# The end of a windowed-attention and MLP kernel: the guard's sum, the last tile's cut and ScalarE's branch

## The chip, the cores and the metric

The kernel runs on one core of a Trainium2 chip. The core has TensorE (matrix multiplication, with its weight loads listed apart), VectorE, ScalarE, GpSimd and SyncE; each has its own queue of instructions and they meet through semaphores. DMAs are issued from the queues of SyncE, ScalarE and GpSimd and run on 16 DMA engines. The metric is device time in microseconds (us), lower is better. Times of single steps come from one profiled execution, in us from the start of its span.

## The reference

Four batches of 768 rows, 8 heads of 64 columns, attention over a window of 128 keys and 4 sink keys, then a layer norm, two matrices with a ReLU between them, and the sum with the attention's output:

```python
keep = is_sink | in_window              # n_sink = 4, window = 128
scores = np.where(keep, scores, -1e9)   # scores = q k^T / 8
a = np.exp(scores - max);  a = a / (sum(a) + 1e-9)
x = (a @ v)                             # heads side by side: [4, 768, 512]
xn = (x - mu) / np.sqrt(var + 1e-6) * g_ln
out = x + np.maximum(xn @ w_ch1, 0) @ w_ch2     # 512 -> 2048 -> 512
```

## The kernel before

The 3072 rows are 24 tiles of 128 rows, handled as 12 chunks of 256. A chunk passes through loads, transposes, scores, exponentials, the product with v, the norm, and the two layers of `mlp(c)`. No maximum is subtracted before the exponential. The kernel instead keeps the reciprocals of all row sums in `rec` (128 x 24 x 8) and at the end counts those outside 1e-9 to 1e9. If the count is zero, the result stands; otherwise the slow routine `general` computes everything again. That count is the **guard**.

The order of the instructions is not written out by hand. Each step is given to a planner as `P.op(name, engines with estimated times, priority, code, reads, writes)`. The planner simulates the engines, gives each step the moment at which its inputs, its engine and its buffers are free, and the steps are then emitted in order of planned start. Each engine works through its own steps in that order. Buffers come from rings; the ring `one` has four PSUM banks, and a step that writes to a new buffer of it must wait until the last user of a bank is done with it.

The end of the program is what the change touches:

- The second layer of a tile is 16 matmuls that add up in one bank, in four steps `pc{t}{f}_{s}` of four (line 1074). VectorE then writes `ot`, the sum with the attention's output (step `o{t}{f}`, line 1083), and a store goes out (line 1087). For the last tile, number 23, the 512 columns are divided by `LAST_CUTS` into two halves with matmuls, sum and store of their own; the first half's store is issued by ScalarE, the second's by SyncE.
- `guard` (lines 1114 to 1116, VectorE) leaves one count for each partition in `n_bad`. `gsum` (line 1119) adds them over the partitions by a matmul with a column of ones into a bank of the ring `one`. `gflag` (line 1121, VectorE) copies the sum as an integer to `flag`.
- `hold` (line 1125) is a matmul that reads the last column of the last output tile. It keeps TensorE from going on before that tile is summed.
- `nc.values_load(flag)` (line 1159) loads the flag into a register of every engine, and `tc.If` (line 1161) has each engine compare and branch over `general`. The last store of SyncE, `order_last`, is emitted behind that load. Hints at the program's start mark the branch as likely taken for TensorE, ScalarE and GpSimd.
- Behind the branch come the waits and barriers that end the program (line 1196 in the trace). SyncE waits there for one semaphore after the other, those of the stores among them.

Of the kernel before, what the change touches and what calls it, by code (L numbers as in the profile page):

```python
# [7 lines left out]
FP32 = mybir.dt.float32  # L8
BF16 = mybir.dt.bfloat16
AF = mybir.ActivationFunctionType  # L10
ALU = mybir.AluOpType
# [185 lines left out]
def pe(us):  # L197
    return {"PE": (us, us + Plan.PE_DRAIN)}


def act(n):
    t = 0.065 + 0.000833 * n
    return (t, t + 0.105)


def dve(n, per=1.04):
    t = 0.067 + 0.001 * per * n
    return (t, t + 0.09)


def fix(occ, extra=0.09):
    return (occ, occ + extra)
# [12 lines left out]
SW_Q = (0.25, 0.7, 0.9)  # L225

LOW, HIGH = 1e-9, 1e9
LAST_CUTS, LAST_ACT = (0, 256, 512), (3,)
NEG = -1e30
NEVER = -1e9  # L230
BIG = 3.3e38
# [138 lines left out]
def kernel(  # L370
# [12 lines left out]
    nc = tc.nc  # L383
# [6 lines left out]
    DM = moe_w_ch1.shape[0]  # L390
# [3 lines left out]
    NT = B * RB  # L394
    NC = B * RC
# [7 lines left out]
    P = Plan()  # L403
# [26 lines left out]
    def const(name, shape, dtype):  # L430
        return consts.tile(shape, dtype, name=name)
# [14 lines left out]
    w2 = [const(f"w2_{c}", [128, 4, DM], BF16) for c in range(4)]  # L446
    junk = nc.const_aps.tensor(1.0, [128, 512], BF16)
    rec, low = const("rec", [128, NT, H], FP32), const("low", [128, NT, H], FP32)
    n_bad, flag = const("n_bad", [128, 1], FP32), const("flag", [1, 1], mybir.dt.int32)
    g_s, g_r = const("g_s", [128, H, NS], FP32), const("g_r", [128, 3, H], FP32)  # L450
    ones_f = const("ones_f", [128, 1], FP32)
# [3 lines left out]
    Bc = {n: Buf(n) for n in names}  # L455
# [4 lines left out]
    def constant(name, eng, us, prio, emit, reads=(), **kw):  # L460
        return P.op(name, {eng: fix(us)}, prio, emit, reads=[Bc[r] for r in reads], **kw)

    V, G = nc.vector, nc.gpsimd
# [4 lines left out]
        out=ident_f, in_=ident_f, compare_op=ALU.not_equal, fill=1.0, base=0,  # L468
        pattern=[[-1, 128]], channel_multiplier=1), rw=[Bc["ident_f"]])
    constant("up1", "POOL", 0.3, -98, lambda e: G.affine_select(  # L470
        out=upper, in_=upper, compare_op=ALU.is_ge, fill=0.0, base=0,
# [36 lines left out]
    def negs(e):  # L508
# [7 lines left out]
        out=sel.rearrange("p (a b h) -> p a b h", a=2, b=2),  # L516
        in_=ident.rearrange("p (a b t h s) -> p t a b h s", a=2, b=2, h=2, s=NS)[:, 0],
        op=ALU.add, axis=mybir.AxisListType.X), ["ident"], writes=[Bc["sel"]])
# [8 lines left out]
         writes=[gr_b], dma=HW_T)  # L527
    P.op("gtt", pe(0.1), PAR["gtt"], lambda e: nc.tensor.transpose(gt_p.t[:, 0:NDM], g_rows, ident_f[0:NDM, 0:NDM]),
         reads=[gr_b, Bc["ident_f"]], writes=[gt_p])
    P.op("gtc", {"DVE": fix(0.07)}, PAR["gtt"] + 0.1, lambda e: V.tensor_copy(gt, gt_p.t[:, 0:NDM]), reads=[gt_p], writes=[Bc["gt"]])  # L530
    for h in range(H):
# [3 lines left out]
            reads=[Bc["vc"]], writes=[Bc["vcd"]], nb=3.5 + 0.55 * h)  # L535
    for b in range(B):
# [4 lines left out]
            reads=[Bc["vcd"], Bc["vc"], Bc["sel4" if b else "sel"]], writes=[Bvs[b]], nb=PAR["vs0"][1] if b == 0 else 40.0 * b)  # L541
# [7 lines left out]
    for c in range(4):  # L549
        sl = slice(512 * c, 512 * (c + 1))  # L550
        P.op(f"w1ld{c}", {"POOL": (0.75, 0.8)}, w1prio[c], lambda e, c=c, sl=sl: G.dma_start(
            w1[c], moe_w_ch1[:, sl].rearrange("(j p) n -> p j n", p=128)), writes=[Bw1[c]], dma=SW_W)
    for c in range(4):
        P.op(f"w2ld{c}", {"POOL": (0.75, 0.8)}, PAR["w2p"][c], lambda e, c=c: G.dma_start(
            w2[c], moe_w_ch2[512 * c:512 * (c + 1), :].rearrange("(t p) n -> p t n", p=128)),
            writes=[Bw2[c]], dma=SW_W)
# [471 lines left out]
    def mlp(c):  # L1028
        T = 16.0 * c + 8.0
# [3 lines left out]
        for u in range(NH1 // 2):  # L1033
# [8 lines left out]
            def mm(e, u=u, ph=ph):  # L1042
                for s in range(2):
                    ht = 2 * u + s
                    for j in range(NDM):
# [4 lines left out]
            o = P.op(f"ph{c}_{u}", pe(0.944 if by_tile else 0.872), pr, mm_t if by_tile else mm, reads=[xnt_t[2 * c + u % 2] if by_tile else xnt, (Bw1 if c < PAR["x_by_dma"] else Bw1g)[u // 2]],  # L1050
                     writes=[ph], hold=[hb, xnt])
# [10 lines left out]
        for i in range(2):  # L1062
            t = 2 * c + i
            b, r = t // RB, t % RB
            ot, st, rs, x = Buf(f"ot{t}", "ot"), xst_b[t], xst_b[t, "rs"], x_b[t]
            cuts = LAST_CUTS if t == NT - 1 else (0, DM)
            for f in range(len(cuts) - 1):
                pc, wd = Buf(f"pc{t}{f}", "one"), cuts[f + 1] - cuts[f]
                sl = slice(cuts[f], cuts[f + 1])
                for s in range(4):  # L1070
                    def mm(e, s=s, i=i, pc=pc, sl=sl, wd=wd):
                        for ii in range(4):
                            ht = 4 * s + ii
                            nc.tensor.matmul(pc.t[:, 0:wd],  # L1074
                                             lhsT=(h1[2 * s + i].t[:, 128 * ii:128 * ii + 128] if by_tile else
                                                   h1[ht // 2].t[:, 256 * (ht % 2) + 128 * i:256 * (ht % 2) + 128 * i + 128]),
                                             rhs=w2[s][:, ii, sl], start=ht == 0, stop=ht == NH1 - 1)
                    P.op(f"pc{t}{f}_{s}", pe(0.865 * wd / DM), T + 4 * i + s + 4 * f + 0.5, mm,
                         reads=[*([h1[2 * s + i]] if by_tile else h1[2 * s:2 * s + 2]), Bw2[s]], **({"writes": [pc]} if s == 0 else {"rw": [pc]}))
                oo = Buf(f"oo{t}{f}")  # L1080
                tail["ot"], tail["oo"] = ot, oo
                P.op(f"o{t}{f}", {"DVE": dve(wd, 1.14)}, T + 4 * i + 3.5, lambda e, sl=sl, pc=pc, wd=wd, ot=ot, st=st, x=x:
                     V.scalar_tensor_tensor(ot.t[:, sl], in0=pc.t[:, 0:wd], scalar=st.t[:, 16:17],  # L1083
                                            in1=x.t[:, sl], op0=ALU.mult, op1=ALU.add),
                     reads=[pc, st, rs, x], writes=[ot, oo])
                P.op(f"st{t}{f}", {"ACT" if len(cuts) - f in LAST_ACT else "SP": (0.54, 0.59)}, T + 4 * i + 3.6,
                     lambda e, sl=sl, ot=ot, b=b, r=r: (nc.sync if e == "SP" else nc.scalar).dma_start(
                         out[b, 128 * r:128 * (r + 1), sl], ot.t[:, sl]),
                     reads=[ot, oo], dma=HW_S)

    last_use, tail = {}, {}
# [11 lines left out]
    for c in range(NC):  # L1103
        mlp(c)
        if c == PAR["x_by_dma"] - 1:
            for s in range(4):
                for j in range(NDM):
# [3 lines left out]
                         reads=[Bw1[s], Bc["gt"]], writes=[Bw1g[s]], after=last_use[s])  # L1111

    def guard(e):
        V.tensor_scalar(low, rec, LOW, HIGH, op0=ALU.max, op1=ALU.min)
        V.tensor_tensor(low, low, rec, op=ALU.not_equal)
        V.tensor_reduce(out=n_bad, in_=low, op=ALU.add, axis=mybir.AxisListType.XY)
    nb_b, pt_f, fl_b = Buf("n_bad"), Buf("ptf", "one"), Buf("flag")
    P.op("guard", {"DVE": fix(0.9)}, 1000.0, guard, reads=recs, writes=[nb_b])
    P.op("gsum", pe(0.06), 16.0 * NC + 0.7, lambda e: nc.tensor.matmul(
        pt_f.t[0:1, 0:1], lhsT=n_bad, rhs=ones_f, start=True, stop=True), reads=[nb_b, Bc["ones_f"]], writes=[pt_f])  # L1120
    P.op("gflag", {"DVE": fix(0.1)}, 1000.0, lambda e: V.tensor_copy(flag, pt_f.t[0:1, 0:1]),
         reads=[pt_f], writes=[fl_b])

    hl = Buf("hold", "one")
    P.op("hold", pe(0.06), 1000.0, lambda e: nc.tensor.matmul(
        hl.t[0:1, 0:1], lhsT=tail["ot"].t[:, DM - 1:DM], rhs=ones_f, start=True, stop=True),
        reads=[tail["ot"], tail["oo"], Bc["ones_f"]], writes=[hl])

    order = P.run()

# [2 lines left out]
    t = PAR["t0"]  # L1133
    for o in order:
# [6 lines left out]
        if n > 0:  # L1141
            free = [(max([e_ for b_, e_ in banks[i].lives if b_ < t], default=0.0), i) for i in range(8)
                    if all(e_ < t or b_ > o.start + 0.3 for b_, e_ in banks[i].lives)]
            if free:
                i = min(free)[1]
                sizes = [512] * (n // 2) + [256] * (n % 2) if cold else [256] * n
                items.append((t + 0.001, -1, (sizes, pairs[i // 2][:, i % 2, :] if i < 4 else ones[i - 4])))
        t = o.start + occ * (2 if cold and not o.name.startswith("pm") else 1)
# [52 lines left out]
```

## Time and profile before

| | |
|---|---|
| time, median of 3 runs | 216.89 us (216.62 to 217.34) |
| the profiled execution: time | 217.02 us |
| the profiled execution: span, first to last instruction | 215.5 us |
| granted TensorE clock | 1.00 throughout |
| TensorE busy | 205.9 us, 96% of the span |
| VectorE, ScalarE, GpSimd busy | 53%, 51%, 52% |

In the rows below PE is TensorE's matmuls, PEld its weight loads, DVE VectorE, ACT ScalarE, POOL GpSimd and SP SyncE. A q behind the name (ACTq) marks an instruction of the engine's sequencer: a wait, a branch, a load of a register, the issue of a DMA. A row of the timeline has start, length, engine, line, operation, output<-inputs, shape and count; in brackets stands the idle time before it and what ended it. A row of a source line has the least, median and greatest length in ns and the first and last start. A matmul's listed length includes its way through the array, so matmuls overlap and their pace is read from their starts.

### The profile page before, as it was taken

The numbers are of one execution on the slowest core, as the hardware profiler recorded it, in microseconds if no ns is written. First come the engines' busy times: TensorE is split into PE (matmuls) and PEld (weight loads), VectorE is DVE, ScalarE is ACT, GpSimd is POOL, SyncE is SP. The second block draws the span as 40 slices with busy tenths as digits, with TensorE's granted clock in tenths as the row PEclk, the third lists the DMA queues.
The fourth block names the chain that finished last, engine by engine and source line by source line (L and its number), as shares of the span: only waits on it lengthen the run. The fifth ranks groups of instructions, "written<-read, shape, count | busy, mean of one in ns | idle before, by whom it ended". The sixth has DMA issues, their size and how long they took to land.

```text
span 215.5 us, 6660 instructions
## 1 busy us (share of the span) xinstructions
PE 205.9 (96%) x2743; PEld 144.1 (67%) x2765; DVE 115.3 (53%) x315; ACT 110.0 (51%) x178; POOL 111.8 (52%) x166
## 2 busy tenths in 40 slices
PE   7798899999999999999999999999999999999994
PEld 2467875765865875864865865864865865865853
DVE  5589875698445446446345446446355345444011
ACT  3796387496562562562562562562562562530610
POOL 7978632499972881871971981871971211201000
PEclk9999999999999999999999999999999999999999
DMA  5999999999999999799799899899799302202103
GB/s 156 187 190 205 193 206 192 167 180 132 154 187 169 123 125 145 87 175 151 123 115 170 112 147 145 111 122 168 111 141 149 80 3 76 73 0 76 49 2 105
DMA packets 104554, 28.04 MB, mean 130 GB/s; under 512 B 94788, under 2 KB 101576, under 8 KB 104520
## 3 DMA queue, kind: packets, MB, share of 16 engines
q0 software_dynamic: 69872, 13.18, 90.2%
q1 hardware_dynamic: 33448, 13.74, 35.7%
q10 hardware_dynamic: 1200, 0.66, 1.1%
q8 instruction: 22, 0.36, 0.7%
q14 instruction: 12, 0.10, 0.2%
HBM read 27.43 MB, written 6.29 MB: 156 GB/s over the span
## 4 chain that ended last, share of the span: by engine, by line
PE 88%; DVE 5%; DMA 3%; issue 2%; ACT 1%; ACTq 0%; DVEq 0%
PE one L1074 39%; PE one L1046 36%; PE pair L980 3%; DMA natf<-in_q_dram 3%; PE one L953 2%; PE one L960 2%; PE one L969 1%; DVE st L881 1%; DVE xnt L909 1%; PE one L988 1%; PE one L1039 1%; DVE x L873 1%; DVE xc L885 1%; PE pair L605 1%; PE pair L730 1%
## 5 line engine op out<-in xcount | busy, mean ns | idle before, releaser
L1074 PE MATMUL one<-w,h 128*128 128x512 bf16 (+1 forms) x378 | 84.5, 371 | 2.2 <-issue 1.6
L1056 ACT ACTIVATE h<-one 128x512 bf16<-128x512 f32 x93 | 55.6, 598 | 47.3 <-PE one L1046 42.6
L1046 PE MATMUL one<-xnt,w 128*128 128x256 bf16 x704 | 79.3, 273 | 0.0
L1046 PEld LDWEIGHTS <-w 128*128 128x128 bf16 x704 | 68.6, 98 | 10.4
L1074 PEld LDWEIGHTS <-h 128*128 128x128 bf16 x400 | 37.3, 98 | 39.6
L998 ACT ACTIVATE pe<-pair 128x768 bf16<-128x768 f32 x36 | 27.2, 809 | 41.0 <-PE pair L980 41.0
L645 POOL DMA_DIRECT2D vn<-in_v_dram x59 | 38.7, 695 | 10.9 <-DMA w<-in_moe_w_ch_dram 6.8
L890 POOL TENSOR_SCALAR st<-st 128x1 f32<-128x1 f32 x24 | 8.9, 369 | 62.4 <-DVE st L883 61.9
L1021 DVE RECIPROCAL rec<-one 128x4 f32<-128x4 f32 x36 | 6.4, 178 | 62.5 <-PE one L969 51.1
L1083 DVE SCALAR_TENSOR_TENSOR ot<-one,st,x 128x512 f32<-128x512 f32 (+1 forms) x25 | 18.2, 727 | 13.9 <-PE one L1074 9.0
L891 POOL TENSOR_TENSOR st<-st,mhalf 128x1 f32<-128x1 f32 x24 | 17.0, 707 | 2.0
L881 DVE BATCH_NORM_STATS2 st<-x 128x6 f32<-128x512 bf16 x24 | 16.7, 695 | 0.8
L1023 DVE TENSOR_TENSOR x<-one,rec 128x256 bf16<-128x256 f32 x36 | 15.3, 425 | 1.2
L703 POOL DMA_DIRECT2D nat<-in_k_dram x16 | 14.9, 932 | 1.9 <-DMA natp<-in_q_dram 1.6
L703 POOL DMA_DIRECT2D nat<-in_q_dram x16 | 14.3, 905 | 0.0
L1003 DVE TENSOR_TENSOR pe<-pe,band 128x768 bf16<-128x768 bf16 x24 | 12.2, 552 | 0.0
L885 DVE TENSOR_SCALAR xc<-x,st 128x512 bf16<-128x512 bf16 x24 | 9.3, 387 | 0.9
L980 PE MATMUL pair<-qT,kT 64*64 64x128 bf16 (+1 forms) x528 | 9.2, 204 | 0.0
L953 PEld LDWEIGHTS <-pe 128*128 128x128 bf16 (+1 forms) x144 | 6.2, 97 | 2.9 <-issue 0.8
L778 ACT ACTIVATE pe<-pair 128x1024 bf16<-128x1024 f32 (+1 forms) x8 | 7.1, 916 | 1.8 <-PE pair L730 1.4
L1039 PE MATMUL one<-xnt,w 128*128 128x128 bf16 x128 | 8.0, 220 | 0.0
L980 PEld LDWEIGHTS <-kT 64*64 64x64 bf16 x528 | 7.2, 108 | 0.4 <-ACT w L1110 0.4
(112 smaller groups left out, 165.7 us busy)
## 6 DMA issues: line engine op xcount, KB each, us to landing
out_dram<-ot SPq DMA_DIRECT2D x23, 256.0 KB
w<-in_moe_w_ch_dram POOLq DMA_DIRECT2D x8, 512.0 KB, 14.5
nat<-in_k_dram POOLq DMA_DIRECT2D x16, 128.0 KB, 5.1
nat<-in_q_dram POOLq DMA_DIRECT2D x16, 128.0 KB, 5.6
vn<-in_v_dram POOLq DMA_DIRECT2D x44, 32.0 KB, 6.0
vn<-in_v_dram POOLq DMA_DIRECT2D x15, 64.0 KB, 6.3
natp<-in_k_dram POOLq DMA_DIRECT2D x3, 256.0 KB, 14.3
vn<-in_v_dram POOLq DMA_DIRECT2D x6, 128.0 KB, 9.2
```

What stands on the lines that cost most here:

```text
L645: P.op(f"vld{t}_{i}", {"POOL": (0.8, 0.85)}, prio + 0.001 * i, lambda e, p0=p0, n=n, hs=hs, src=src: G.dma_start(m.t[p0:p0 + n, hs, 0:64], ...
L703: lambda e, nat=nat, ap=ap: G.dma_start(nat.t, ap), writes=[nat], dma=SW, after=gate(c))
L881: P.op(f"bn{t}", {"DVE": fix(0.60)}, d + 0.12, lambda e: V.bn_stats(st.t[:, 8:14], x.t), reads=[x], writes=[st, mv])
L891: G.tensor_tensor(st.t[:, 16:17], st.t[:, 17:18], mhalf, op=ALU.pow)),
L980: nc.tensor.matmul(pps[u].t[64 * g:64 * g + 64, h2, col + c0:col + c0 + n], lhsT=kt.t[rs, hp, k0:k0 + 64], rhs=qT.t[rs, hp, q0:q0 + n], st ...
L998: nc.scalar.activation(pes[j].t.rearrange("p a b -> p (a b)")[:, 0:768].rearrange("p (a b) -> p a b", a=2), pps[j].t[:, :, 0:384], AF.Exp, ...
L1003: V.tensor_mul(at_s, at_s, band[j] if r > 1 else edge[r][j].unsqueeze(1).to_broadcast([128, 4, 192]))
L1023: P.op(f"x{t - 1}{u}", {"DVE": dve(256)}, d + 0.051 + 0.002 * u, lambda e, u=u, rc=rc, pv=pv: V.tensor_tensor(x.t[:, 256 * u:256 * u + 256 ...
L1046: nc.tensor.matmul(ph.t[:, 256 * s:256 * s + 256], lhsT=w1[ht // 4][:, j, 128 * (ht % 4):128 * (ht % 4 + 1)], rhs=xnt.t[:, j, :], start=j ...
L1056: nc.scalar.activation(hb.t, ph.t, AF.Relu)
L1074: nc.tensor.matmul(pc.t[:, 0:wd], lhsT=(h1[2 * s + i].t[:, 128 * ii:128 * ii + 128] if by_tile else h1[ht // 2].t[:, 256 * (ht % 2) + 128 ...
L1083: V.scalar_tensor_tensor(ot.t[:, sl], in0=pc.t[:, 0:wd], scalar=st.t[:, 16:17], in1=x.t[:, sl], op0=ALU.mult, op1=ALU.add),
```

## The change

Three things are changed, all at the end of the program.

1. The guard's counts are no longer added by TensorE. A DMA issued by GpSimd (`gmove`) moves the 128 counts from 128 partitions into one row of one partition, and VectorE reduces that row and copies it to `flag` (`gflag`). This step is placed behind the sum of tile 22 (`after=[tail["sum", NT - 2]]`).
2. The last tile's second layer is divided at column 320 instead of 256: the first part has 320 columns, the second 192.
3. ScalarE gets a copy of one element of the last output tile (`hold_act`), behind which its load of the flag and its branch stand.

```diff
-LAST_CUTS, LAST_ACT = (0, 256, 512), (3,)
+LAST_CUTS, LAST_ACT = (0, 320, 512), (3,)
...
+    n_bad_t, n_sum, act_end = const("n_bad_t", [1, 128], FP32), const("n_sum", [1, 1], FP32), const("act_end", [1, 1], FP32)
...
-                P.op(f"o{t}{f}", {"DVE": dve(wd, 1.14)}, T + 4 * i + 3.5, lambda e, sl=sl, pc=pc, wd=wd, ot=ot, st=st, x=x:
+                tail["sum", t] = P.op(f"o{t}{f}", {"DVE": dve(wd, 1.14)}, T + 4 * i + 3.5, lambda e, sl=sl, pc=pc, wd=wd, ot=ot, st=st, x=x:
...
-    nb_b, pt_f, fl_b = Buf("n_bad"), Buf("ptf", "one"), Buf("flag")
+    nb_b, fl_b = Buf("n_bad"), Buf("flag")
     P.op("guard", {"DVE": fix(0.9)}, 1000.0, guard, reads=recs, writes=[nb_b])
-    P.op("gsum", pe(0.06), 16.0 * NC + 0.7, lambda e: nc.tensor.matmul(
-        pt_f.t[0:1, 0:1], lhsT=n_bad, rhs=ones_f, start=True, stop=True), reads=[nb_b, Bc["ones_f"]], writes=[pt_f])
-    P.op("gflag", {"DVE": fix(0.1)}, 1000.0, lambda e: V.tensor_copy(flag, pt_f.t[0:1, 0:1]),
-         reads=[pt_f], writes=[fl_b])
+    nt_b = Buf("n_bad_t")
+    P.op("gmove", {"POOL": (0.8, 0.85)}, 1000.0, lambda e: G.dma_start(n_bad_t[0:1, :], n_bad[:, 0:1]),
+         reads=[nb_b], writes=[nt_b], dma=SW_Q)
+    def total(e):
+        V.tensor_reduce(out=n_sum, in_=n_bad_t, op=ALU.add, axis=mybir.AxisListType.X)
+        V.tensor_copy(flag, n_sum)
+    P.op("gflag", {"DVE": fix(0.2)}, 1000.0, total, reads=[nt_b], writes=[fl_b], after=[tail["sum", NT - 2]])
...
+    P.op("hold_act", {"ACT": act(1)}, 1001.0, lambda e: nc.scalar.copy(act_end, tail["ot"].t[0:1, DM - 1:DM]),
+         reads=[tail["ot"], tail["oo"]], writes=[Buf("hold_act")])
```

## The prediction

> **What bounds the kernel now.** I read the page first (engines, chain), then the chain of waits and the timeline of the last 11 us, then the rows of the exit (flag loads, branches, end waits), then the DMA shares of that stretch.
>
> ```profile
> span 215.5 us, 6660 instructions
> PE 205.9 (96%) x2743; PEld 144.1 (67%) x2765; DVE 115.3 (53%) x315; ACT 110.0 (51%) x178; POOL 111.8 (52%) x166
> PE 88%; DVE 5%; DMA 3%; issue 2%; ACT 1%; ACTq 0%; DVEq 0%
> ```
>
> TensorE is busy 96% of the span and carries 88% of the chain. The diff touches nothing ahead of the guard's counting (L1116 at 194.3 us), so every term lies in the end. The timeline there, in order (start, length, engine, line):
>
> ```profile
> 194.01 0.69 POOL L891 TENSOR_TENSOR st<-st,mhalf 128x1 f32<-128x1 f32 x1
> 194.32 0.35 DVE L1116 TENSOR_REDUCE n_bad<-low 128x1 f32<-128x192 f32 x1
> 195.78 2.32 PE L1074 MATMUL one<-w,h 128*128 128x512 bf16 x10
> 197.94 7.15 PE L1046 MATMUL one<-xnt,w 128*128 128x256 bf16 x64
> 205.19 0.60 ACT L1056 ACTIVATE h<-one 128x512 bf16<-128x512 f32 x1 [0.28 <-PE one L1046]
> 205.36 0.60 PE L1074 MATMUL one<-w,h 128*128 128x512 bf16 x2
> 205.88 0.09 PEld L1119 LDWEIGHTS one<-ones_f,n_bad 128*1 128x1 f32 x2 [0.42 <-ACT h L1056]
> 206.01 6.26 PE L1074 MATMUL one<-w,h 128*128 128x512 bf16 x44
> 206.11 0.15 DVE L1121 CAST flag<-one 1x1 int32<-1x1 f32 x1 [7.16 <-PE one L1119]
> 208.86 0.75 DVE L1083 SCALAR_TENSOR_TENSOR ot<-one,st,x 128x512 f32<-128x512 f32 x1 [2.61 <-PE one L1074]
> 210.72 0.48 DVE L1083 SCALAR_TENSOR_TENSOR ot<-one,st,x 128x256 f32<-128x256 f32 x1 [1.11 <-PE one L1074]
> 211.24 0.38 ACTq L1087 DMA_DIRECT2D out_dram<-ot  x1
> 212.37 0.48 DVE L1083 SCALAR_TENSOR_TENSOR ot<-one,st,x 128x256 f32<-128x256 f32 x1 [1.16 <-PE one L1074]
> 212.88 0.34 SPq L1087 DMA_DIRECT2D out_dram<-ot  x1
> ```
>
> TensorE runs without a gap to 212.27 except around the guard's matmul (L1119); the last sum, `o231`, follows, and SyncE issues the last store at 212.88. What comes behind it is in the rows of the exit: flag loads (L1159), branches (L1161), end waits (L1196; its SyncE row asked for in two stretches).
>
> ```profile
> L1159 POOLq TENSOR_LOAD <-flag x1: 498/498/498, 206.3 to 206.3; - x1
> L1159 SPq TENSOR_LOAD <-flag x1: 516/516/516, 210.0 to 210.0; - x1
> L1159 SPq SEQ_ASSERT  x1: 37/37/37, 210.8 to 210.8; - x1
> L1159 ACTq TENSOR_LOAD <-flag x1: 473/473/473, 211.7 to 211.7; - x1
> L1161 ACTq COMPARE_BRANCH  x1: 68/68/68, 212.2 to 212.2; - x1
> L1161 ACTq EVENT_SEMAPHORE  x1: 17/17/17, 212.7 to 212.7; - x1
> L1196 ACTq DRAIN  x1: 8/8/8, 212.8 to 212.8; - x1
> L1196 POOLq DRAIN  x1: 1380/1380/1380, 208.3 to 208.3; - x1
> L1196 SPq EVENT_SEMAPHORE  x11: 28/28/28, 213.8 to 214.4; - x11
> L1196 SPq EVENT_SEMAPHORE  x1: 28/28/28, 214.6 to 214.6; - x1
> L1196 SPq DRAIN  x1: 13/13/13, 214.7 to 214.7; - x1
> L1196 POOLq EVENT_SEMAPHORE  x4: 17/17/17, 214.8 to 215.4; - x4
> ```
>
> SyncE makes twelve end waits. Eleven run from 213.8 to 214.4, 0.06 us apart; the twelfth, for the last store, is at 214.6 and not 214.5. SyncE drains at 214.7, GpSimd's barrier follows at 214.8, the span ends at 215.5. ScalarE was there at 212.8, GpSimd at 208.3 + 1.4 = 209.7. So the end is set by last sum, last store and SyncE's waits, and those two have slack.
>
> **The change, part by part.**
>
> *The guard's matmul goes.* The two matmuls ahead of it end at 205.96. One of 512 columns lasts 0.38 (row below), so the second began at 205.58. They start 0.216 apart ((2.32 - 0.38)/9 in the row of 195.78), so the next would begin at 205.80; it began at 206.01. Saved: 0.21. The guard's weight load waited for ScalarE's 205.19 + 0.60 = 205.79, which frees the PSUM bank it wrote to. The matmul behind it accumulates in a bank already held, on hidden blocks written long ago. If it had to wait for that same release, it would start at 205.88, where the guard's load did: 0.13 saved. Bounds 0.13 to 0.22; a loss is excluded, since TensorE gets no instruction in place of these. I take 0.21, because that wait belongs to the bank.
>
> *Cut at 320.* TensorE's time for the last tile must not grow: 16 matmuls of 320 and 16 of 192 for 32 of 256.
>
> ```profile
> L1074 PE MATMUL one<-w,h x378: 272/379/391, 30.9 to 212.0; 128*128 128x512 bf16 x173, 128*128 128x256 bf16 x16
> 22.77 1.95 PE L1039 MATMUL one<-xnt,w 128*128 128x128 bf16 x32
> ```
>
> The row of L1074 holds the lengths: 272 ns is the 256-column one, 379 the 512. Starts are 0.109 apart at 256 columns ((7.15 - 0.27)/63), 0.216 at 512: 0.42 ns a column. At 128 they are at most 0.061 apart (1.95/32), so the weight loads, one a matmul, allow at least that and 192 columns take 0.082 by the line, 0.085 at most (midway between 0.061 and 0.109). Old and new are both 3.49 us; at worst 16 x 0.003 = 0.05 is lost. I take 0, since the line holds to within 0.008 at 128. The last sum shrinks: 0.75 at 512 and 0.48 at 256 columns is 1.04 ns a column, so 64 fewer save 0.07 (bounds 0.05 to 0.08 by the rounding of the rows). The first sum moves 16 x 64 x 0.42 ns = 0.43 later and is 0.07 longer: from 210.72 - 0.21 + 0.43 = 210.94 to 211.49. ScalarE's store issue, 0.38, then ends at 211.9; nothing waits for it before the end. `o231` starts at 212.16 and ends at 212.58, the store is issued at 212.61 instead of 212.88.
>
> *A smaller last store*, 96 for 128 KB. The DMA shares by stretch (the last two numbers are the share and GB/s):
>
> ```profile
> 213.25:213.65 0.40, 0.00 (x0) 0.00 (x0) 0.00 (x0) 0.00 (x0) 0.00 (x0) 1.00 0.05 20
> 213.65:214.25 0.60, 0.00 (x0) 0.00 (x0) 0.00 (x0) 0.00 (x0) 0.00 (x0) 1.00 0.71 232
> 214.70:215.50 0.80, 0.00 (x0) 0.00 (x0) 0.00 (x0) 0.00 (x0) 0.00 (x0) 1.00 0.11 20
> ```
>
> The store's packets fill 213.65 to 214.25; a quarter less is at most 0.15. SyncE can use only the 0.1 by which its twelfth wait is late; after that its own row of waits is next. Bounds 0 to 0.1. I take 0.08, near the upper end, as the byte share exceeds it.
>
> *GpSimd's DMA, and VectorE's sum and copy.* `n_bad` is ready at 194.67, GpSimd free at 194.70. Its other small DMAs:
>
> ```profile
> L645 POOL DMA_DIRECT2D vn<-in_v_dram x59: 610/677/829, 29.9 to 159.1; - x59
> DMA to landing us min/median/max: 4.0/6.1/13.3
> ```
>
> So GpSimd spends 0.6 to 0.9 and the row lands between 198.7 and 208.0. Nothing stands behind it on GpSimd but the flag load. VectorE takes it up behind the sum of tile 22, which now ends at 209.61 - 0.21 = 209.40. The reduction of 128 elements lies between the cast (0.15) and the reduction of 192 (0.35), the copy is 0.15: flag at 209.7 to 209.9. VectorE is idle there for 1.11, now 1.54. SyncE loads the flag at about 209.9 as before and is through in 0.85; its store comes at 212.6. GpSimd's exit lasts 206.3 to 209.7, 3.4, so it ends at 213.3; the barrier wants it at 214.3. Cost 0, hidden by 0.9 us of slack. Without that cover each microsecond by which the flag is late costs one.
>
> *ScalarE behind a copy.* A copy of one element: 0.2 (row below), no second table load in the run, though casts, Exp and Relu all ran.
>
> ```profile
> L474 ACT ACT_TABLE_LOAD x1 | 1.3, 1283 | 2.2 <-issue 2.2
> L474 ACT ACTIVATE one_e<-one_e 128x1 f32<-128x1 f32 x1 | 0.2, 203 | 0.0
> q8 instruction: 22, 0.36, 0.7%
> q14 instruction: 12, 0.10, 0.2%
> ```
>
> It waits for 212.58. Behind it stand only flag load and branch: from load (211.7) to drain (212.8) 1.1 us, so 213.7, against 214.3. Cost 0, 0.6 us of cover. The branch also moves bytes: in 213.25 to 213.65 there are 20 GB/s x 0.4 = 8 KB that are no store, the size of a q14 packet (0.10 MB/12), 1.0 us behind ScalarE's branch. That would move to about 214.2, past the store's packets (now 213.4 to 213.9). Bounds: such a packet takes 0.2% x 16 x 215.5/12 = 0.57 of an engine, so 0.57 lost to 0.57 won; nothing in the rows shows anyone waiting for one, so 0.
>
> A rule that speaks against this step is in the Trainium skill, "Runtime: NRT & Kernel Launch", section on instruction fetch: a taken branch to a page not held must fetch it before it goes on. The trace disagrees for ScalarE's present branch: the next instruction comes 0.5 us later, while the 8 KB arrive after 1.0.
>
> Sum: 0.21 + 0.07 + 0.08 = 0.36. The profiled execution took 217.02, of which 215.5 are the span and 1.5 lie around it, so 216.66. It lies 0.13 above the median of the three runs, 216.89, so against that 216.53; I say 216.5.
>
> **Rivals.** 0.3% (0.65 us) is about what a measurement of this kernel can tell from no change.
> 1. *The flag comes late* (the other side). If the transfer lands after 210.5 us instead of by 208.0, VectorE, in order, holds the flag's sum and both last sums behind it; or if the flag is made only behind the first sum (211.49 + 0.45 = 211.94), GpSimd's 3.4 us end at 215.35 instead of before 214.76. It decides from a flag at 210.9 on (214.3 - 3.4). Price of the second: 0.59 on 217.02, 217.5 against the median; of the first, 1 us per us. For: only loads of 32 KB and more are seen on this queue, none this scattered. Against: 2.5 us of margin, and the traffic beside it is the output's stores alone. 0.15.
> 2. *ScalarE becomes last.* Should its branch now wait for its bytes, 0.8 (a store's issue at 212.88 to its packets at 213.65) + 0.57 instead of 0.5, it drains at 214.6 and the gain shrinks to about 0.1: 216.8. 0.12. This is also what the rule above would make of it.
> 3. *The part behind the span shrinks too.* 16 KB of instructions run at 214.7 to 215.5 and 1.5 us follow. A q8 packet holds an engine for 0.7% x 16 x 215.5/22 = 1.1. If the exit waits for it and it is freed of the others, 0.3 to 0.6 more: 216.1. For: the bytes are there. Against: with ScalarE's bytes moved towards them it may be the reverse. 0.27.
>
> **How the numbers follow.** The forecast has 0.46, own range 216.2 to 216.8 (the bounds, plus the runs' spread). Faster by over 0.3% is rival 3 and the forecast's low edge: 0.27 + 0.08 = 0.35. Slower is rival 1: 0.15 (its cheaper form ends at the edge of that class, a late landing well beyond). The rest, 0.50, is within. For 8 in 10 the range goes down to 215.8 (all but the lower tail of rival 3) and up to 217.4 (just short of rival 1).
>
> **What would show it.** TensorE: no gap at 205.8, last matmul ending near 212.05. The last sum 0.42 long, ending near 212.6. SyncE's drain 214.3 to 214.4, span near 215.2. The flag made before the first last sum; GpSimd's long drain ending near 213.3. I am wrong if ScalarE or GpSimd reaches the barrier behind SyncE, if VectorE waits for the small transfer, or if matmuls of 192 columns start more than 0.083 apart.

## The result and the profile after

| | before | after |
|---|---|---|
| time, median of 22 runs each | 216.74 us (216.53 to 218.29) | 216.21 us (216.02 to 217.71) |
| the profiled execution: time, span | 217.02, 215.5 us | 216.10, 214.6 us |

The ratio is 0.9977, with a 95% interval of 0.9968 to 0.9987: 0.5 us less, between 0.3 and 0.7, so a small gain inside the 0.3% that was called no change. Here and below a ratio and its interval come from all executions of both kernels, so a ratio need not be the quotient of the two medians. The forecast was 216.5 us, 0.36 less than before.

The two profiled executions differ by 0.92, but most of that has nothing to do with the change. ScalarE's last ReLU, the last thing ahead of the second layer of the last two tiles, starts at 205.19 before and at 204.63 after, so 0.56 is gone earlier than anything that was altered. Of it 0.15 is there by 19 us, where loads at the program's start landed earlier, and 0.41 comes in one place. The timeline of the kernel before:

```profile
24.46 0.87 POOL L627 DMA_DIRECT2D vn<-in_v_dram  x1 [1.57 <-DMA w<-in_moe_w_ch_dram]
24.67 0.76 DVE L885 TENSOR_SCALAR xc<-x,st 128x512 bf16<-128x512 bf16 x1
```

and of the kernel after:

```profile
24.49 0.88 POOL L628 DMA_DIRECT2D vn<-in_v_dram  x1 [1.64 <-DMA w<-in_moe_w_ch_dram]
24.52 0.35 DVE L886 TENSOR_SCALAR xc<-x,st 128x512 bf16<-128x512 bf16 x1
```

The same operation of VectorE lasts 0.76 where it starts 0.21 behind the start of GpSimd's issue of a DMA (it ends at 25.43, the issue at 25.33), and 0.35 where it starts 0.03 behind it. Of the thirteen profiles of this document (before, after and the runs below) only the one of before has the long operation at this place. Three kernels below have the old program unaltered up to the guard, `cut_only`, `pair_bank` and `hold_only`. Their last ReLU starts at 204.48, 204.63 and 204.72, so single profiles lie 0.2 apart even without it, and 0.7 apart with it. So from here on all moments are counted from the start of the last ReLU, and what comes behind it is called the tail.

The page after, its span, engines and chain:

```profile
span 214.6 us, 6660 instructions
PE 206.0 (96%) x2741; PEld 144.3 (67%) x2763; DVE 115.2 (54%) x316; ACT 110.1 (51%) x179; POOL 111.7 (52%) x167
PE 88%; DVE 5%; DMA 2%; issue 2%; ACT 1%; SPq 0%; DVEq 0%
```

TensorE has two matmuls fewer (the guard's one fp32 matmul counts as two) and is as busy as before. The timeline of the tail (lines are one to six higher than before):

```profile
204.37 7.11 PE L1075 MATMUL one<-w,h 128*128 128x512 bf16 x47
204.63 0.60 ACT L1057 ACTIVATE h<-one 128x512 bf16<-128x512 f32 x1 [0.28 <-PE one L1047]
208.08 0.75 DVE L1084 SCALAR_TENSOR_TENSOR ot<-one,st,x 128x512 f32<-128x512 f32 x1 [9.69 <-PE one L1075]
208.75 0.27 DVE L1125 TENSOR_REDUCE n_sum<-n_bad_t 1x1 f32<-1x128 f32 x1
208.86 3.51 SPq L1088 DMA_DIRECT2D out_dram<-ot  x2
209.04 0.14 DVE L1126 CAST flag<-n_sum 1x1 int32<-1x1 f32 x1
210.36 0.55 DVE L1084 SCALAR_TENSOR_TENSOR ot<-one,st,x 128x320 f32<-128x320 f32 x1 [1.18 <-POOLq L1167]
211.59 0.42 DVE L1084 SCALAR_TENSOR_TENSOR ot<-one,st,x 128x192 f32<-128x192 f32 x1 [0.67 <-PE one L1075]
212.04 0.19 ACT L1132 COPY act_end<-ot 1x1 f32<-1x1 f32 x1 [6.81 <-DVE ot L1084]
```

The matmuls stand in one group, where the guard's two split them before. The sum of tile 22 comes 208.08 - 204.63 = 3.45 behind the ReLU, 208.86 - 205.19 = 3.67 before. The flag is made at 209.18, ahead of the last tile's two sums. SyncE's two issues end at 208.86 + 3.51 = 212.37, so the last store is issued at 212.37 - 0.34 = 212.03. The rows of the guard's DMA (L1121), of the branch (L1167) and of the end (L1202; SyncE's asked for in three stretches):

```profile
L1121 POOL DMA_DIRECT2D n_bad_t<-n_bad x1: 646/646/646, 194.4 to 194.4; - x1
DMA to landing us min/median/max: 2.1/2.1/2.1
L1167 ACTq COMPARE_BRANCH  x1: 68/68/68, 212.6 to 212.6; - x1
L1202 SPq EVENT_SEMAPHORE  x11: 28/28/28, 213.0 to 213.6; - x11
L1202 SPq EVENT_SEMAPHORE  x1: 28/28/28, 213.7 to 213.7; - x1
L1202 SPq DRAIN  x2: 7/10/13, 213.7 to 213.8; - x2
L1202 POOLq DRAIN  x1: 1457/1457/1457, 211.3 to 211.3; - x1
L1202 ACTq DRAIN  x2: 8/8/8, 213.2 to 214.0; - x2
```

The guard's row landed after 2.1 us, 12 us before VectorE took it up. GpSimd is through at 211.3 + 1.5 = 212.8 and ScalarE at 213.2, both ahead of SyncE's drain at 213.7, and the end is still SyncE's. By the trace's times, which are finer than the rows:

| behind the start of the last ReLU, us | before | after | difference | forecast |
|---|---|---|---|---|
| sum of tile 22 starts | 3.68 | 3.45 | -0.23 | -0.21 |
| last sum ends | 7.67 | 7.38 | -0.29 | -0.28 |
| last store issued | 7.69 | 7.40 | -0.29 | -0.28 |
| last store landed, on the last of its DMA engines | 9.39 | 9.02 | -0.37 | |
| SyncE's wait for it | 9.41 | 9.03 | -0.38 | -0.36 |
| end of the span | 10.35 | 9.98 | -0.37 | -0.36 |

### The profile page after: what moved, and what is told of

Same layout as the page of the kernel before. It is cut to its first block, busy times and chain, and to the rows that moved or that the text cites. A ratio compares the mean times of both kernels' runs of the same rounds, so it can differ in the third digit from the quotient of the medians.

```text
span 214.6 us, 6660 instructions
## 1 busy us (share of the span) xinstructions
PE 206.0 (96%) x2741; PEld 144.3 (67%) x2763; DVE 115.2 (54%) x316; ACT 110.1 (51%) x179; POOL 111.7 (52%) x167
## 4 chain that ended last, share of the span: by engine, by line
PE 88%; DVE 5%; DMA 2%; issue 2%; ACT 1%; SPq 0%; DVEq 0%
PE one L1075 39%; PE one L1047 36%; PE pair L981 3%; DMA natf<-in_k_dram 2%; PE one L954 2%; PE one L961 2%; PE one L970 1%; DVE st L882 1%; DVE xnt L910 1%; PE one L989 1%; PE one L1040 1%; DVE x L874 1%; PE pair L606 1%; PE pair L731 1%; DVE pe L782 1%
## 5 line engine op out<-in xcount | busy, mean ns | idle before, releaser
L1075 PE MATMUL one<-w,h 128*128 128x512 bf16 (+2 forms) x378 | 84.3, 370 | 2.2 <-issue 1.6
L891 POOL TENSOR_SCALAR st<-st 128x1 f32<-128x1 f32 x24 | 8.4, 349 | 62.7 <-DVE st L884 62.0
L1084 DVE SCALAR_TENSOR_TENSOR ot<-one,st,x 128x512 f32<-128x512 f32 (+2 forms) x25 | 18.2, 727 | 20.6 <-PE one L1075 14.5
L886 DVE TENSOR_SCALAR xc<-x,st 128x512 bf16<-128x512 bf16 x24 | 8.7, 364 | 0.9
```

Of the source, the lines that this page charges most:

```text
L1075: nc.tensor.matmul(pc.t[:, 0:wd], lhsT=(h1[2 * s + i].t[:, 128 * ii:128 * ii + 128] if by_tile else h1[ht // 2].t[:, 256 * (ht % 2) + 128 ...
```

## The experiments

Three questions were open: whether the pause of the guard's matmul is what the prediction took it for, whether the three parts add up, and whether the two steps that were costed at nothing (ScalarE's copy, GpSimd's flag) are nothing. In the theory that the prediction states they add: 0.21, 0.15 for cut and smaller store, 0, 0. The rival is that an engine's branch sets off a transfer of instructions that shares a DMA engine with the last store, so that what counts is *when* each engine branches.

**The guard's part alone.** The kernel before with part 1 of the change, cut at 256 and no copy on ScalarE:

```diff
-    P.op("gsum", ...)        # matmul into the ring "one"
+    P.op("gmove", ...)       # GpSimd's DMA
...
+    P.op("gflag", {"DVE": fix(0.2)}, 1000.0, total, reads=[nt_b], writes=[fl_b], after=[tail["sum", NT - 2]])
```

> The kernel before with the first part of the change alone (the guard's counts by a DMA and VectorE; cut at 256, ScalarE's branch as before). The end is measured from the start of ScalarE's last ReLU, which both kernels reach unchanged: last store issued 7.69 us behind it before and 7.40 after, span ending 10.3 behind it before and 10.0 after. Theory (the terms of the forecast): only TensorE's pause of 0.22 goes, so the store is issued at 7.46 to 7.48 and the span ends at 10.1; time about 0.2 below before. Rival (the medians of before and after lie 0.53 apart and the forecast's terms explain 0.37, so the first part shortens something outside the end as well): same end, time 0.35 to 0.4 below before.

216.50 us against 216.71 of the kernel before on that chip, ratio 0.9997 (0.9982 to 1.0013), an interval that holds both no change and the 0.21, so the time alone settles nothing. In the tail the pause is gone: the sum of tile 22 at 3.45 instead of 3.68, the last store issued at 7.47 instead of 7.69. But the span's end comes only 0.08 earlier, because the store landed 1.83 behind its issue and not 1.70. Fifteen DMA engines were done by 9.16, the sixteenth at 9.30. ScalarE's 8 KB of instructions, set off by its branch at 6.79, run at 7.88 to 8.35, and the store's packets begin at 8.30. So the term of 0.21 stands for the issue of the store, most of it was lost again behind it, and the run left it open whether a transfer of instructions can hold the store up.

**What the pause is.** The kernel before, with the guard's matmul writing to a bank of another ring, which no one uses at that time:

```diff
-    nb_b, pt_f, fl_b = Buf("n_bad"), Buf("ptf", "one"), Buf("flag")
+    nb_b, pt_f, fl_b = Buf("n_bad"), Buf("ptf", "pair"), Buf("flag")
```

> The kernel before, the guard's matmul writing to a bank of the ring pair, free since the last scores, instead of the ring one. TensorE's pause around the guard's matmul, from the start of the last matmul before it to the start of the next, was 0.43, against 0.216 without it. Theory (the pause is mostly the wait for the bank that ScalarE's last ReLU frees): the matmul starts 0.1 earlier and only its own 0.12 is left, 0.34 in all; store issue at 7.60 instead of 7.69. Rival (the pause is the matmul's own, with the change of type and shape): 0.43 and 7.69 as before.

216.69 against 216.59, ratio 1.0006 (0.999 to 1.0022). Its timeline:

```profile
204.37 1.03 PE L1074 MATMUL one<-w,h 128*128 128x512 bf16 x3
204.63 0.60 ACT L1056 ACTIVATE h<-one 128x512 bf16<-128x512 f32 x1 [0.28 <-PE one L1046]
205.32 0.09 PEld L1119 LDWEIGHTS pair<-ones_f,n_bad 128*1 128x1 f32 x2 [0.42 <-issue]
205.44 1.25 PE L1074 MATMUL one<-w,h 128*128 128x512 bf16 x5
```

The third matmul starts at 204.37 + 1.03 - 0.38 = 205.02 and the fourth at 205.44: 0.42 to 0.43 apart, as in the kernel before (205.58 to 206.01), where 0.216 is the pace. So the theory on record (a pause of 0.34, the store issued at 7.60) falls and its rival holds. There is no bank to wait for any more, and the weight load's idle time is the same 0.42, now put down to "issue" and not to ScalarE's ReLU. The pause is the cost of the fp32 matmul with its weight load between two bf16 ones. That the ReLU ended just ahead of the load was a coincidence, and the releaser in the row of before was an inference that happened to fit.

**The change without ScalarE's copy.**

```diff
-    P.op("hold_act", {"ACT": act(1)}, 1001.0, lambda e: nc.scalar.copy(act_end, tail["ot"].t[0:1, DM - 1:DM]),
-         reads=[tail["ot"], tail["oo"]], writes=[Buf("hold_act")])
```

> The changed kernel without ScalarE's copy; its flag load then stands behind its own store issue alone (load about 6.7 behind the last ReLU, branch 7.3). Theory (the forecast's 0 for this step): nobody waits for the bytes of that branch, store issue at 7.40, SyncE's twelfth end wait 0.06 behind the eleventh, span end at 10.0, time as the changed kernel's. Rival (collision): the 8 KB that come about 1.0 behind the branch, at 8.3, fall among the last store's packets (8.2 to 8.8) and hold one of the 16 engines for 0.3 to 0.6; the store lands later, the twelfth wait comes 0.1 to 0.5 later and the span ends at 10.1 to 10.5.

217.00 against 216.71, ratio 1.001 (0.9999 to 1.002): the gain is gone, and whether the kernel is slower than the one before the interval leaves open. The last store is issued at 7.40 as in the kernel after, but the span's end is at 11.12 instead of 9.98, later than even the rival on record had it (10.1 to 10.5). The rows of its branch and of SyncE's end waits:

```profile
L1165 ACTq COMPARE_BRANCH  x1: 68/68/68, 212.0 to 212.0; - x1
L1200 SPq EVENT_SEMAPHORE  x11: 27/28/28, 213.1 to 213.7; - x11
L1200 SPq EVENT_SEMAPHORE  x1: 28/28/28, 214.9 to 214.9; - x1
```

The twelfth wait, for the last store, is 1.2 behind the eleventh. Why, the DMA rates in slices of 0.05 us show, from 8.1 to 10.1 behind the last ReLU. First the kernel after (212.73 to 214.73):

```profile
GB/s 0 0 77 184 292 353 338 307 262 123 31 0 0 0 0 0 328 0 0 0 0 0 328 0 164 0 0 0 0 0 0 0 0 0 0 0 0 0 0 0
```

then the one without the copy (212.84 to 214.84):

```profile
GB/s 0 0 46 154 292 292 323 292 246 169 31 0 0 0 164 164 164 0 0 0 15 343 31 15 15 0 0 15 0 15 0 0 0 0 0 0 0 0 0 0
```

A packet of the last store is 96 KB / 128 = 768 bytes, 15 GB/s in such a slice; 8 KB of instructions are 164, 16 KB 328. (A transfer is booked where it starts.) After, all 128 packets are through by the eleventh slice, and the instructions follow. Without the copy three transfers of 8 KB come first, and behind them stand eight store packets one by one (15, the 15 in 343, two in 31, and four of 15): the whole share of one DMA engine. Fifteen engines had landed by 9.01, this one at 10.14. The first of the eight starts at 9.13, where the first block of instructions (8.83 to 9.14) ends. In `cut_only` and `late_flag` below, the last eight start at 9.13 and 9.04, where the blocks of ScalarE and GpSimd end (9.13 and 9.05). So the late share is that of the engine that carries the block. Why that engine moved nothing for the store between 8.24, when the others began, and 8.83 the records don't say. So a copy of 0.19 us on ScalarE is worth 0.8 us between the medians (217.00 to 216.21) and 1.14 between the two tails, and the theory that the parts add falls.

**The cut alone.** The kernel before with the last tile divided at 320.

```diff
-LAST_CUTS, LAST_ACT = (0, 256, 512), (3,)
+LAST_CUTS, LAST_ACT = (0, 320, 512), (3,)
```

> The kernel before with the cut at 320 alone; the guard's matmul stays and ScalarE has no copy. Forecast's term for this part by itself: 0.15 less, span end 10.2 behind the last ReLU. Theory (collision, from the run without the copy): the later first sum moves ScalarE's store issue and so its branch 0.5 later, to 7.5, only 0.05 ahead of the last store's issue at 7.6; its 8 KB then fall among the store's packets, one of the 16 engines lands about 1.1 later, the twelfth wait comes at 10.3 to 10.4, span end 11.3, time 0.5 to 0.9 above before. Rival (the collision needs GpSimd's late branch too): span end 10.2.

217.16 against 216.59, ratio 1.0025 (1.0009 to 1.004): slower. The last sum ends 0.07 earlier, as forecast, but the span's end comes 0.41 later. The longer first sum moves ScalarE's store and with it its branch from 7.01 to 7.50. The DMA rates from 8.1 to 10.1 behind its last ReLU (212.58 to 214.58):

```profile
GB/s 0 0 0 0 0 0 0 108 246 486 323 307 246 215 62 16 0 0 0 0 179 31 15 31 15 15 492 0 0 0 0 0 0 0 0 0 0 0 0 0
```

ScalarE's 8 KB stand in the tenth slice, in the midst of the store's packets; the last eight packets of 768 bytes come from the 21st on (179 is one of them with 8 KB). The store lands at 9.80, 2.17 behind its issue. The cause is the one seen above; that theory's number, a tail of 11.3, was too high (10.76).

**The copy alone, and with the guard's part.** The kernel before with the copy and nothing else:

```diff
+    P.op("hold_act", {"ACT": act(1)}, 1001.0, lambda e: nc.scalar.copy(act_end, tail["ot"].t[0:1, DM - 1:DM]),
+         reads=[tail["ot"], tail["oo"]], writes=[Buf("hold_act")])
```

> The kernel before with ScalarE's copy alone. Forecast's term for this part: 0. Theory (collision): in the kernel before ScalarE's 8 KB come at 8.1 to 8.4 or 8.6 behind the last ReLU and the store's packets at 8.5; its last engine landed at 9.39 in one profile, and at 9.59 in the kernel with the guard's matmul in another bank, whose end is otherwise the same. So some executions lose 0.1 to 0.3. With the copy the store lands at 9.3 to 9.4, the span ends at 10.3, the time is about 0.15 below before and its executions lie closer together. Rival (the copy only matters with the cut at 320): span end 10.35, time as before within 0.05.

216.50 against 216.62, ratio 0.9989 (0.9973 to 1.0005). The tail is that of the profiled execution before, 10.35. The 0.12 would fit executions of the kernel before that lose something to ScalarE's 8 KB now and then, but the interval includes no change.

The kernel after with the cut back at 256, so the guard's part with the copy:

```diff
-LAST_CUTS, LAST_ACT = (0, 320, 512), (3,)
+LAST_CUTS, LAST_ACT = (0, 256, 512), (3,)
```

> The changed kernel with the cut back at 256: the guard's part and ScalarE's copy. Measured from the start of ScalarE's last ReLU. With the guard's part alone the store was issued at 7.47, its last packet engine landed at 9.30 and SyncE's twelfth wait came at 9.31, span end 10.27. Theory (collision): without the copy ScalarE's 8 KB went over one DMA engine at 7.9 to 8.4, just ahead of the store's packets, and held them there; with the copy they move behind the store, the store lands 1.70 behind its issue as before, at 9.17, twelfth wait at 9.2, span end at 10.1, time 0.1 to 0.15 below the guard's part alone. Rival (the late landing has another cause): span end 10.27 as without the copy.

216.31 against 216.59, ratio 0.9983 (0.9973 to 0.9993). Beside the guard's part alone the store is issued at the same 7.47, but lands 1.69 and not 1.83 behind its issue, and the tail is 10.12 and not 10.27.

**Is it the branch, or when its bytes come?** The kernel after without the copy, and with both stores of the last tile on SyncE, so that ScalarE has nothing to do at the end and branches early:

```diff
-LAST_CUTS, LAST_ACT = (0, 320, 512), (3,)
+LAST_CUTS, LAST_ACT = (0, 320, 512), ()
...
-    P.op("hold_act", {"ACT": act(1)}, 1001.0, lambda e: nc.scalar.copy(act_end, tail["ot"].t[0:1, DM - 1:DM]),
-         reads=[tail["ot"], tail["oo"]], writes=[Buf("hold_act")])
```

> The changed kernel without ScalarE's copy and with the first part's store moved from ScalarE's queue to SyncE's, so that ScalarE has nothing to wait for and branches as soon as the flag is there, at 5.2 behind the last ReLU. SyncE's load of the flag now stands behind that store, so the last store is issued at about 7.55 instead of 7.40. Theory (what costs is where the 8 KB fall, not that ScalarE has no copy): they come at 6.2, long before the last store's packets; the store lands 1.62 behind its issue, twelfth wait at 9.2, span end at 10.1, time 0.1 to 0.2 above the changed kernel. Rival (ScalarE must not branch before the last store whatever the time): twelfth wait at 10, span end at 11, as in the run without the copy.

216.48 against 216.62, ratio 0.9995 (0.9985 to 1.0004). ScalarE branches at 209.9:

```profile
L1165 ACTq COMPARE_BRANCH  x1: 68/68/68, 209.9 to 209.9; - x1
```

That is 5.12 behind the ReLU; its bytes are one of two blocks of 8 KB at 6.27 to 6.79 (the other is that of GpSimd, which branches at 5.17), ahead of the last store, which lands 1.62 behind its issue as in the kernel after. So ScalarE may branch early or late, but not between: a branch at 7.28 or 7.50 costs, and with one at 6.79 (`gsum_only`) or 7.01 (`pair_bank`) a store landed late too. The kernel is 0.31 slower than the one after on the same chip (216.17, below), for an expected 0.1 to 0.2. Of that 0.25 is in the tail, where SyncE's load of the flag now stands between two stores and the last is issued at 7.65.

**Another engine's branch.** The kernel after without `hold` on TensorE, ScalarE's copy kept:

```diff
-    hl = Buf("hold", "one")
-    P.op("hold", pe(0.06), 1000.0, lambda e: nc.tensor.matmul(...)
```

> The changed kernel without TensorE's matmul on the last output tile (ScalarE's copy stays), so TensorE loads the flag and branches as soon as its last matmul is handed on, 0.5 to 0.9 earlier. Theory (all branches' transfers share DMA engines with the store): its 16 KB, which take 0.9 to 1.4, come at 8.1 to 8.5 behind the last ReLU instead of 9.2, among the store's packets (8.2 to 8.7); the store lands up to 1 later and the span ends at 10.3 to 11. Rival (only the small transfers share an engine with the store): span end 9.9 to 10.0, time as the changed kernel's.

217.12 against 216.59, ratio 1.002 (1.0009 to 1.0031). TensorE's branch and the rows of SyncE's waits:

```profile
L1163 PEldq COMPARE_BRANCH  x1: 398/398/398, 210.6 to 210.6; - x1
L1198 SPq EVENT_SEMAPHORE  x2: 28/28/28, 214.6 to 214.8; - x2
```

TensorE branches at 5.89 behind the ReLU and its 16 KB run from 7.05 to 8.60, a microsecond earlier than expected, but still into the store's packets. Two waits are late, the last at 10.11: both parts of the last tile's store had a DMA engine that lay behind these bytes (landing at 9.86 and 10.09). So `hold` and `hold_act` do the same, each for the bytes of its engine.

**A later cut.** The kernel after, divided at 384:

```diff
-LAST_CUTS, LAST_ACT = (0, 320, 512), (3,)
+LAST_CUTS, LAST_ACT = (0, 384, 512), (3,)
```

> The changed kernel with the last tile divided at column 384. Theory: matmuls of 128 columns start 0.056 apart, so TensorE's time is unchanged; the last sum is 64 columns shorter, 0.07; the first sum grows to 0.62 and ends 0.1 to 0.2 before the last one can start; the store shrinks to 64 KB, which gains nothing since SyncE's own row of end waits is next. Store issue at 7.33, span end 0.07 earlier than at 320. Rival 1 (the store's landing still ends the program): 0.07 + 0.08 earlier. Rival 2 (the longer first sum holds up the last one): no gain or a loss of up to 0.1.

216.20 against 216.71, ratio 0.9979 (0.9969 to 0.9989). The last sum is 0.07 shorter again, but with the store of 64 KB landing 1.63 behind its issue, no sooner than that of 96 KB (1.62), the tail is only 0.03 shorter. That shows no floor, for the two stores of the last tile meet here: the first part's, 192 KB now, moves packets until 8.39, the last store's run from 8.22 to 8.60. In the kernel after, those of the first part end at 7.79, ahead of the last store's. So this cut gains nothing more, and what a smaller store alone would bring stays untested.

**A late flag.** The kernel after with the flag made behind the first of the last tile's sums instead of behind tile 22's:

```diff
-    ... writes=[fl_b], after=[tail["sum", NT - 2]])
+    ... writes=[fl_b], after=[tail["sum", NT - 1, 0]])
```

> The changed kernel with the flag's sum and copy placed behind the first sum of the last tile instead of behind tile 22's. The flag is then made about 2.15 us later (6.7 behind the last ReLU, before 4.56). Theory (the first rival of the prediction, second form): GpSimd's exit takes 3.55 us from the flag, ends at 10.25 and the barrier waits for it, where SyncE would be there at 9.2 to 9.4; the span ends at 11.0 to 11.1, time 1.0 to 1.1 above the changed kernel. Rival (GpSimd's long drain is not of fixed length but shrinks when it comes late): only SyncE's load of the flag, 0.85 long and ahead of the last store, is late: store issue at 7.6, span end at 10.2, time 0.2 above.

217.23 against 216.71, ratio 1.0029 (1.0019 to 1.0039). The flag is made at 6.64 instead of 4.56. GpSimd's and SyncE's rows at the end:

```profile
L1202 POOLq DRAIN  x3: 46/103/1457, 213.8 to 215.8; - x3
L1202 SPq DRAIN  x2: 7/10/13, 214.8 to 214.9; - x2
```

GpSimd's long drain runs from 213.8 to 215.2, SyncE is there at 214.8, so GpSimd sets the end, as the first rival said: its exit takes 10.21 - 6.64 = 3.57 from the flag on, and the tail is 11.05. SyncE is late here too (9.83 instead of 9.11), because its own load of the flag puts the last store's issue at 7.57, 0.17 later, and because GpSimd's 8 KB fall among the store's packets (8.37 to 9.05) and the store lands 2.16 behind its issue, at 9.73.

**The change once more**, the same program beside `hold_only` and `act_early` on one chip.

> The changed kernel once more, beside the copy alone on one chip. Theory: span end 10.0 behind the last ReLU, time 0.5 below before: 0.37 of terms in the end and about 0.15 for the collision that the kernel before has in a part of its executions. Rival (the part beyond the terms was chance of the first comparison): 0.35 to 0.4 below.

216.17 against 216.62, ratio 0.9979 (0.997 to 0.9988); tail 9.99.

All tails together, in us behind the last ReLU. "Bytes nearest to it" are blocks of instructions that overlap the packets of the last store or come next to them. The trace doesn't say whose they are; an engine is named where its branch is the one that the block follows:

| kernel | store issued | its packets | bytes nearest to it | landed | behind issue | span's end |
|---|---|---|---|---|---|---|
| before | 7.69 | 8.52 to 9.04 | ScalarE 8.10 to 8.43 | 9.39 | 1.70 | 10.35 |
| `hold_only` | 7.69 | 8.52 to 9.04 | 9.01 to 9.49 | 9.40 | 1.71 | 10.35 |
| `pair_bank` | 7.69 | 8.52 to 9.18 | ScalarE 8.09 to 8.63 | 9.59 | 1.90 | 10.54 |
| `cut_only` | 7.63 | 8.45 to 9.39 | ScalarE 8.59 to 9.13 | 9.80 | 2.17 | 10.76 |
| `gsum_only` | 7.47 | 8.30 to 8.86 | ScalarE 7.88 to 8.35 | 9.30 | 1.83 | 10.27 |
| `sum_and_hold` | 7.47 | 8.29 to 8.82 | 8.81 to 9.36 | 9.16 | 1.69 | 10.12 |
| `no_act_hold` | 7.40 | 8.24 to 9.63 | 8.83 to 9.46, three | 10.14 | 2.74 | 11.12 |
| `no_pe_hold` | 7.40 | 8.24 to 9.64 | TensorE 7.05 to 8.60 | 10.09 | 2.69 | 11.06 |
| `late_flag` | 7.57 | 8.40 to 9.31 | GpSimd 8.37 to 9.05 | 9.73 | 2.16 | 11.05 |
| `act_early` | 7.65 | 8.48 to 8.92 | 8.88 to 9.46 | 9.27 | 1.62 | 10.23 |
| `cut384` | 7.34 | 8.22 to 8.60 | 8.79 to 9.23 | 8.97 | 1.63 | 9.95 |
| after | 7.40 | 8.23 to 8.67 | 8.91 to 9.35 | 9.02 | 1.62 | 9.98 |

A store whose packets no block of instructions meets lands 1.69 to 1.71 behind its issue at 128 KB and 1.62 at 96 KB. Where a block starts over 0.1 ahead of the end of its packets it is 1.83 to 2.74, unless the block ends before the first packet (before, by 0.09). In `no_act_hold` that end is itself late: the other fifteen engines were through at 8.67, ahead of the first block at 8.83. Each row is one profiled execution.

## Why the prediction was right, and where its reasons were not

**The guard's matmul: the size right, the reason wrong.** Forecast 0.21, measured 0.23 in the tail, in the kernel after and in `gsum_only`. (The medians of `gsum_only` are 0.21 apart as well, but its profiled end is only 0.08 earlier and its interval includes zero, so they confirm nothing.) The step said that the pause belongs to the wait for the PSUM bank that ScalarE's ReLU frees. `pair_bank` takes that wait away and the pause stays at 0.42 to 0.43 against a pace of 0.216. The lower bound of 0.13, which came from that reading, was no bound.

**The cut on TensorE and VectorE: right.** No cost on TensorE: the matmuls of 192 columns start 0.0825 apart, where the forecast's line gave 0.082. The last sum is 0.42 long, for 0.48 (rows 211.59 and 212.37), and 0.06 of it shows in the tail (forecast 0.07). The first sum ends at 210.91, ahead of the last as forecast.

**The smaller store: right, near the upper bound as taken.** 0.08: 1.70 to 1.62 from issue to landing. The reason, that SyncE's own row of waits comes next, holds: the twelfth wait is now 0.07 behind the eleventh (8.96 to 9.03), which is their pace. The store landed at 9.02, so it is no longer clearly the later of the two.

**GpSimd's and VectorE's flag: right, with more cover than said.** The row landed after 2.1 us, below the bounds of 4.0 to 13.3 that came from far larger loads. VectorE made the flag directly behind tile 22's sum. GpSimd's exit ended at 8.11, 1.0 ahead of SyncE's drain. The rival's price is confirmed by `late_flag`: 0.59 over the kernel before were put for a flag behind the first sum, 0.52 were measured (217.23 - 216.71; 0.70 between the tails), and GpSimd's exit takes 3.57 from the flag where 3.4 were put. That GpSimd's bytes would delay the store as well wasn't in it.

**ScalarE's copy: the net right, the step wrong.** The step costed the copy at nothing because nothing in the rows showed anyone waiting for the 8 KB that ScalarE's branch moves, with 0.57 either way as the bound. In `no_act_hold` one DMA engine's share of the last store waits for such bytes, and the copy is worth 0.8 us, outside that bound. The step asked what the copy adds to the kernel before, where ScalarE branches at 7.01 and its bytes end just ahead of the store. It didn't ask what the cut does to that branch: with the longer first sum it moves to 7.28 to 7.50, and the bytes move into the store. The cut's own terms, 0.07 + 0.08, are therefore right only with the copy beside it. Alone the cut costs 0.57 us (`cut_only`). The forecast summed parts that don't add, and came out right because all of them were there. As far as the reasons of this step go, that is luck.

The rule that was weighed at this step, in the Trainium skill, "Runtime: NRT & Kernel Launch", section "Instruction fetch mechanics", is that a taken branch must fetch a page that isn't held before it goes on. It isn't seen at work in these runs: in the kernel after ScalarE branches at 212.6 and drains at 213.2, while the transfers of instructions that follow come at 8.91 and later, that is from 213.5 on. Whether the page was held already the records don't say.

What does bear on the collision stands in the Trainium skill, "DMA: Bandwidth & Descriptors", section "Queues, rings and completion order": each DMA engine takes turns between its queues, a whole packet at a time, and such a packet holds several descriptors. The records agree as far as the late engine of `no_pe_hold` goes: it moves the eight transfers that are left of the first part's store (8.59 to 9.37), and only then all eight of the last one (9.38 to 9.64), which the other engines began at 8.24. Eight transfers of the last store take 0.27 us and a block of instructions 0.3 to 1.6, so where the block goes first, taking turns is no protection.

**The rivals.** The flag wasn't late and ScalarE not last. The part behind the span didn't shrink: 217.02 - 215.5 and 216.10 - 214.6 are both 1.5.

**What stays open.** The tail explains 0.37; the medians differ by 0.53, or 0.45 in the repeat. In steps, each between its median and that of the kernel before on its chip: the guard's part 0.21, with the copy 0.28, with the cut 0.45 to 0.53. So the copy may bring 0.07 to 0.12 that the two profiles don't show, from executions of the kernel before in which ScalarE's bytes touch the store, as in the profile of `pair_bank` (landed 1.90 behind issue, tail 10.54). No interval here separates that from zero. Open too is what kept one DMA engine from the store between 8.24 and 8.83 in `no_act_hold`. The collisions are read from one profiled execution of each kernel; the larger ones (`no_act_hold`, `no_pe_hold`, `cut_only`, `late_flag`) show in the medians as well, the smaller ones (`gsum_only`, `pair_bank`) only in the profile.

## What to carry to other kernels

Where several engines branch at the end of a program, look at when the bytes of each branch move, here 1.1 us or more behind it, and keep them out of the time of the last store: hold the branch behind the last output, or let it go well earlier: ScalarE's 2.5 us ahead of the last store's issue was early enough (`act_early`), TensorE's 1.5 us ahead was not (`no_pe_hold`). Price two edits together when one of them moves an instruction that the other one holds; a step costed at nothing needs a run without it. And a releaser in a row is an inference from what ended last: change the thing it names before building on it.

## What the runs showed that was not expected

- The transfers of instructions behind a branch start 1.1 to 1.6 us after it, as far as a block can be put to a branch, and last 0.3 to 0.7 us (8 KB) and 0.9 to 1.6 us (TensorE's 16 KB). They hold up one sixteenth of a store, and the store counts as landed only with its last sixteenth: up to 1.1 us late.
- One fp32 matmul of one column between bf16 matmuls costs TensorE 0.21 us beyond their pace, with no PSUM bank to wait for (`pair_bank`).
- A store of 64 KB landed no sooner behind its issue than one of 96 KB, 1.63 and 1.62 us. Its packets met those of the store before it, so this shows no floor.
- VectorE's 0.35 us operation took 0.76 when it began 0.21 us into GpSimd's issue of a DMA. It happens again elsewhere, here in the kernel after:

```profile
42.78 0.89 POOL L704 DMA_DIRECT2D nat<-in_k_dram  x1 [1.46 <-DMA natp<-in_q_dram]
43.17 0.60 DVE L886 TENSOR_SCALAR xc<-x,st 128x512 bf16<-128x512 bf16 x1
```

In the thirteen traces this operation begins inside such an issue 51 times. The 18 that began at least 0.2 behind the issue's start and at least 0.3 ahead of its end took 0.39 to 0.78, and all 18 ended 0.09 behind the issue. The other 33 took 0.35 or 0.36. The Trainium skill, "SBUF — State Buffer", section "SBUF: two separate sides", has the two engines share a port pair that one holds for a whole instruction while the other is blocked. The traces agree in that the operation is held to a fixed point near the issue's end, but not for the whole issue: those that began in its first 0.13 or last 0.22 ran at full pace. The cause is inferred, since no run took the DMA away. At 24.67 the delay reaches the last ReLU, 0.41, more than the change's 0.37 in the tail; the long operation above doesn't move it.
